# Finishing the very last output tile by column halves

The kernel's very last output tile (128 rows of 384 columns) is computed, evacuated and stored in two halves of 192 columns instead of in one piece. Everything before that tile is as it was.

## The chip, the cores and the metric

One core of a Trainium2 chip; the runs of one set share a chip, the sets were made on four different ones. The metric is the device time in microseconds of one execution; medians are of all runs, ratios of fast runs only.

## The reference, cut to what matters

```python
# attention part: gated linear recurrence, (4, 8, 768, 48) -> x of 3072 tokens x 384
for t in range(S):
    state = f[:, :, t, :, None] * state + outer(k[:, :, t], v[:, :, t])
    y[:, :, t] = q[:, :, t] @ state
# mixture part: 4 experts, 384 -> 1024 -> 384, weights p per token
for e in range(E):
    h = np.maximum(x @ w1[e], 0.0)
    out += p[:, e:e + 1] * (h @ w2[e])
```

## The kernel before

A planner places every step on an engine in simulated time and emits the instructions in that order. For each chunk of 4 x 128 tokens and each expert it computes h (8 blocks of 128 features) and then, per tile of 128 tokens, the output: 8 accumulating matmuls of 384 columns in two groups of 4, one evacuation on VectorE that adds p times the product to the tile, and, after the last expert, one store.

```python
def mm_o(c, e, nt, half):
    for fc in range(half * 4, half * 4 + 4):
        nc.tensor.matmul(out=tl("op", c, e, nt)[:, 0:Din], lhsT=tl("h", c, e)[:, fc, nt * T:(nt + 1) * T],
                         rhs=w2_sb[:, e, fc, :], start=(fc == 0), stop=(fc == KF - 1))
...
        nc.vector.scalar_tensor_tensor(out=o, in0=op, scalar=pe, in1=o, op0=ALU.mult, op1=ALU.add)
...
def store(c, nt):
    r0 = nt * S + c * T
    nc.sync.dma_start(out=out[r0:r0 + T, :], in_=tl("o", c, nt))
...
# the planner: a step whose predecessor ran on the same engine waits its lag + 0.05 us
t = max(t, d.end + d.lag + (self.LATENCY if d.engine != e else 0.05))
...
# a filler matmul is issued for every 0.2 us or so in which TensorE would idle before the first h
for _ in range(o.pad):
    nc.tensor.matmul(out=spare[:, 0:256], lhsT=busy[:, 0:128], rhs=busy, start=True, stop=True)
```

Of the kernel before, what the change touches and what calls it, by code (L numbers as in the profile page):

```python
# [99 lines left out]
def kernel(  # L100
# [11 lines left out]
    nc = tc.nc  # L112
    B, H, S, D = q.shape
    assert (B, H, S, D) == (4, 8, 768, 48)
    T = 128
    C = S // T
# [4 lines left out]
    E, Din, F = moe_w1.shape  # L121
    KD = Din // 128
    KF = F // 128
# [12 lines left out]
    P = Plan(rooms)  # L136
# [14 lines left out]
    for nm, nb in (("gp", 2), ("qk", 2)):  # L151
# [6 lines left out]
        out=mask01, in_=mask01, compare_op=ALU.is_ge, fill=0.0,  # L158
# [13 lines left out]
    w2_sb = wpool.tile([128, E, KF, Din], BF16)  # L172
# [17 lines left out]
    def tl(kind, *key):  # L190

        if (kind, key) not in tiles:
            room = kind if kind in rooms else "ps_m" if kind in ("hp", "op") else "ps_t"
            slot = P.slot[(room, kind) + key if room.startswith("ps_") else (room,) + key]
            if room in ("gp", "qk"):
                tiles[kind, key] = pads[room, slot]
            else:
                shape, dt = shapes[kind]
                pool = ps if room.startswith("ps_") else wk
                tiles[kind, key] = pool.tile(shape, dt, name=f"{room}{slot}")  # L200
        return tiles[kind, key]
# [149 lines left out]
        else:  # L351
            nc.scalar.activation(out=dst, in_=src, func=AF.Relu)  # L352

    def mm_o(c, e, nt, half):
        for fc in range(half * 4, half * 4 + 4):
            nc.tensor.matmul(out=tl("op", c, e, nt)[:, 0:Din], lhsT=tl("h", c, e)[:, fc, nt * T:(nt + 1) * T],  # L356
                             rhs=w2_sb[:, e, fc, :], start=(fc == 0), stop=(fc == KF - 1))

    def ev_o(c, e, nt, eng):
        op, o = tl("op", c, e, nt)[:, 0:Din], tl("o", c, nt)  # L360
        pe = pn[:, nt * C + c, e:e + 1]
        if e > 0:
            nc.vector.scalar_tensor_tensor(out=o, in0=op, scalar=pe, in1=o, op0=ALU.mult, op1=ALU.add)  # L363
        elif eng == "ACT":
            nc.scalar.activation(out=o, in_=op, func=AF.Copy, scale=pe)  # L365
        else:
            nc.vector.tensor_single_scalar(out=o, in_=op, scalar=pe, op=ALU.mult)  # L367

    def store(c, nt):
        r0 = nt * S + c * T  # L370
        nc.sync.dma_start(out=out[r0:r0 + T, :], in_=tl("o", c, nt))


    ld = {}
# [96 lines left out]
    hdone, omm, oev = {}, {}, {}  # L471
# [10 lines left out]

    def add_o(c, e, nt, half):
        p = unit[0] + 0.5
        key = ("ps_m", "op", c, e, nt)
        d = [hdone[k] for k in hdone if k[:2] == (c, e) and half * 4 <= k[2] < half * 4 + 4 and k[3] <= nt * T]
        m = omm[c, e, nt] = P.add(f"o {c}.{e}.{nt}.{half}", {"PE": 0.645}, lambda _: mm_o(c, e, nt, half), p,
                                  deps=d + [wd[e, 2], omm.get((c, e, nt))], takes=[key], lag=0.2, frees=[("h", c, e)])
        if half == 1:
            ev = oev[c, e, nt] = P.add(f"ev_o {c}.{e}.{nt}", {"ACT": 0.58, "DVE": 0.56} if e == 0 else {"DVE": 0.62},  # L490
                                       lambda g: ev_o(c, e, nt, g), p - 1, deps=[m, oev.get((c, e - 1, nt)), pdone[c]],
                                       takes=[("o", c, nt)], frees=[key])
            if e == E - 1:
                P.add(f"store {c}.{nt}", {"DMA": 0.6}, lambda _: store(c, nt), p, deps=[ev], frees=[("o", c, nt)])

    attention(0, lambda b, s: -200 + 3.6 * b + s * 0.8, 1)
    ALL, LO, HI = list(range(B)), [0, 1], [2, 3]
# [2 lines left out]
    def zip_units(hs, os):  # L500
        for i in range(max(len(hs), len(os))):
            if i < len(hs):
                add_h(*hs[i])
            if i < len(os):
                add_o(*os[i])
            unit[0] += 1
# [7 lines left out]
    pdone = []  # L514
# [71 lines left out]
```

## Time and profile before

The time before is 305.67 us (median). The profiled run has a span of 303.5 us.

| what | before | how to read it |
|---|---|---|
| TensorE busy | 97% | the bound up to the last matmul |
| first h matmul | 23.04 us | ends the phase of loads and of filler matmuls |
| first evacuation of the second-to-last pair | 296.75 us | I call all up to here the front |
| from there to the end | 6.78 us | the tail, all that the change touches |

I call the last four tiles A, B, C and D. The tail holds the evacuations of A and B, then those of C and D, and their stores. The view `--windows` from the start of A's evacuation gives the tail to 0.01 us (window, length, then busy times).

```profile
296.75:303.53 6.78, 3.21 (x20) 1.72 (x18) 2.48 (x4) 0.00 (x0) 0.00 (x0) 1.00 0.32 116
```

### The profile page before, as it was taken

How to read it: one execution, taken by the hardware profiler on the slowest of the kernel's cores; microseconds unless marked ns; L12 is line 12 of the kernel's file. 1: busy time of each engine (PE TensorE's matmuls, PEld its weight loads, DVE VectorE, ACT ScalarE, POOL GpSimd, SP SyncE). 2: the span in 40 equal slices, each digit the busy share in tenths (PEclk: the TensorE clock that was granted, in tenths of full speed). 3: DMA queues.
4: the chain of work that ended last, by engine and by line, in shares of the span. 5: the costliest groups of instructions: out<-in, count | busy, mean ns of one | idle time of the engine just before them, and what ended most of it. 6: DMA issues, size and time to landing. Idle time of an engine off the chain costs nothing.

```text
span 303.5 us, 5499 instructions
## 1 busy us (share of the span) xinstructions
PE 294.5 (97%) x2104; PEld 170.5 (56%) x2135; DVE 137.8 (45%) x272; ACT 170.7 (56%) x295; POOL 95.7 (32%) x157
## 2 busy tenths in 40 slices
PE   7899999999999999999999999999999999999995
PEld 5665555567775655455555555555555555555552
DVE  6684013788853764516555344544423443201223
ACT  5767654957865444676356475345476444475430
POOL 4585200408656237423426243522432000000000
PEclk9999999999999999999999999999999999999999
DMA  7999999955993589776997877301322201100002
GB/s 156 204 185 208 208 206 190 225 90 91 215 208 82 111 165 181 170 144 120 189 178 136 213 142 151 51 13 37 92 59 51 48 14 41 73 5 2 0 0 104
DMA packets 137210, 36.08 MB, mean 119 GB/s; under 512 B 128480, under 2 KB 135648, under 8 KB 137184
## 3 DMA queue, kind: packets, MB, share of 16 engines
q1 hardware_dynamic: 131424, 29.45, 48.8%
q0 software_dynamic: 5760, 6.29, 12.5%
q8 instruction: 16, 0.26, 0.4%
q14 instruction: 10, 0.08, 0.1%
HBM read 31.51 MB, written 4.72 MB: 119 GB/s over the span
## 4 chain that ended last, share of the span: by engine, by line
PE 90%; DMA 4%; DVE 2%; POOL 1%; issue 1%; ACT 1%; DVEq 0%; ACTq 0%; POOLq 0%
PE ps_m L356 40%; PE ps_m L344 40%; DMA w_sb<-in_moe_w_dram 3%; PE ps_t L300 2%; PE ps_t L255 1%; PE ps_t L315 1%; PE ps_t L321 1%; PE ps_t L311 1%; PE ps_t L285 1%; DMA f<-in_f_logit_dram 1%; POOL qk L276 1%; PE ps_m L551 1%; DVE qk L276 1%; DVE o L363 0%; DVE AT L304 0%
## 5 line engine op out<-in xcount | busy, mean ns | idle before, releaser
L352 ACT ACTIVATE h<-ps_m 128x512 bf16<-128x512 f32 (+1 forms) x171 | 98.4, 578 | 102.7 <-PE ps_m L344 92.5
L356 PE MATMUL ps_m<-w_sb,h 128*128 128x384 bf16 x768 | 153.0, 326 | 0.2
L344 PE MATMUL ps_m<-xT,w_sb 128*128 128x512 bf16 (+1 forms) x593 | 150.4, 362 | 1.9 <-DVE o L367 0.3
L356 PEld LDWEIGHTS <-h 128*128 128x128 bf16 x768 | 72.5, 98 | 57.4
L363 DVE SCALAR_TENSOR_TENSOR o<-ps_m,pn,o 128x384 f32<-128x384 f32 x72 | 44.4, 617 | 97.2 <-PE ps_m L356 89.8
L344 PEld LDWEIGHTS <-w_sb 128*128 128x128 bf16 x624 | 59.8, 98 | 46.9 <-issue 0.7
L276 POOL TENSOR_TENSOR qk<-q,e 128x384 bf16<-128x384 f32 x19 | 22.8, 1203 | 66.7 <-ACT e L262 66.2
L304 DVE TENSOR_TENSOR AT<-ps_t,mask 128x512 bf16<-128x512 f32 x48 | 31.1, 685 | 19.3 <-PE ps_t L300 19.2
L335 POOL TENSOR_TENSOR Sf<-Sf,egs 48x192 f32<-48x192 f32 x40 | 20.4, 510 | 47.5 <-DVE Sf L328 45.5
L350 DVE TENSOR_SCALAR h<-ps_m 128x512 bf16<-128x512 f32 (+1 forms) x37 | 20.7, 573 | 22.0 <-PE ps_m L344 19.7
L276 POOL TENSOR_TENSOR qk<-k,e 128x384 bf16<-128x384 f32 x20 | 21.3, 1064 | 20.3 <-ACT e L264 13.0
L262 ACT ACTIVATE e<-ps_t 128x384 f32<-128x384 f32 x24 | 20.7, 864 | 4.6 <-PE ps_t L255 2.4
L328 DVE TENSOR_TENSOR Sf<-Sf,ps_t 48x192 f32<-48x192 f32 x40 | 14.0, 350 | 9.4 <-PE ps_t L321 8.7
L336 POOL CAST sb<-Sf 48x192 bf16<-48x192 f32 x40 | 13.6, 339 | 2.6
L551 PE MATMUL ps_m<-busy 128*128 128x256 bf16 x71 | 13.1, 332 | 1.3 <-DVE busy L140 1.3
L365 ACT ACTIVATE o<-ps_m,pn 128x384 f32<-128x384 f32 x20 | 11.6, 581 | 3.9 <-PE ps_m L356 3.1
L264 ACT ACTIVATE e<-ps_t 128x384 f32<-128x384 f32 x24 | 13.0, 541 | 0.0
L218 DVE CAST yb<-ps_t 128x384 bf16<-128x384 f32 x16 | 8.9, 556 | 7.3 <-PE ps_t L315 6.3
L247 ACT ACTIVATE ex<-f 128x768 f32<-128x768 f32 (+1 forms) x14 | 10.5, 747 | 3.0 <-DMA f<-in_f_logit_dram 3.0
L315 PE MATMUL ps_t<-vb,AT 128*128 128x48 bf16 x192 | 11.4, 184 | 0.7 <-DVE vb L218 0.7
L315 PEld LDWEIGHTS <-AT 128*128 128x128 bf16 x192 | 9.8, 97 | 2.8 <-issue 0.9
L251 ACT ACTIVATE gp<-ex 128x768 bf16<-128x768 f32 (+1 forms) x14 | 10.5, 751 | 0.4
(50 smaller groups left out, 142.6 us busy)
## 6 DMA issues: line engine op xcount, KB each, us to landing
w_sb<-in_moe_w_dram POOLq DMA_DIRECT2D x8, 768.0 KB, 18.6
out_dram<-o SPq DMA_DIRECT2D x24, 192.0 KB, 1.9
f<-in_f_logit_dram SPq DMA_DIRECT2D x10, 384.0 KB, 4.2
k<-in_k_dram SPq DMA_DIRECT2D x10, 384.0 KB, 5.3
q<-in_q_dram SPq DMA_DIRECT2D x10, 384.0 KB, 5.3
v<-in_v_dram SPq DMA_DIRECT2D x10, 384.0 KB, 5.5
f<-in_f_logit_dram SPq DMA_DIRECT2D x4, 192.0 KB, 3.8
k<-in_k_dram SPq DMA_DIRECT2D x4, 192.0 KB, 3.9
```

Of the source, the lines that this page charges most:

```text
L262: nc.scalar.activation(out=e[:, 0].rearrange("t (d h) -> t h d", d=D), in_=cs[:, 0:HD].rearrange("t (i r d) -> t r i d", r=2, d=D), func=A ...
L276: engines[eng].tensor_tensor(out=tl("qk", c, b)[:, j, :, 0:D].rearrange("t (i r) d -> t i r d", r=2), in0=tl("qk"[j], c, b // 2)[:, hh(b), ...
L304: nc.vector.tensor_tensor(out=tl("AT", c, b)[:, r].rearrange("s i t -> s (i t)"), in0=tl("A", c, b, r).rearrange("s i t -> s (i t)"), in1= ...
L315: nc.tensor.matmul(out=y[:, h * D:(h + 1) * D], lhsT=AT[:, r, i, :], rhs=vb[:, h, :], start=(c == 0), stop=True, skip_group_check=True)
L328: nc.vector.tensor_tensor(out=Sf[rows, b], in0=Sf[rows, b], in1=KV[rows, :, r, :], op=ALU.add)
L335: nc.gpsimd.tensor_tensor(out=Sf[rows, b], in0=Sf[rows, b], in1=eg, op=ALU.mult)
L344: nc.tensor.matmul(out=tl("hp", c, e, fc, n0)[:, n0:n1], lhsT=w1_sb[:, e, kk, fc * 128:(fc + 1) * 128], rhs=tl("xT", c)[:, kk, n0:n1], sta ...
L350: nc.vector.tensor_relu(out=dst, in_=src)
L352: nc.scalar.activation(out=dst, in_=src, func=AF.Relu)
L356: nc.tensor.matmul(out=tl("op", c, e, nt)[:, 0:Din], lhsT=tl("h", c, e)[:, fc, nt * T:(nt + 1) * T], rhs=w2_sb[:, e, fc, :], start=(fc == ...
L363: nc.vector.scalar_tensor_tensor(out=o, in0=op, scalar=pe, in1=o, op0=ALU.mult, op1=ALU.add)
L551: nc.tensor.matmul(out=spare[:, 0:256], lhsT=busy[:, 0:128], rhs=busy, start=True, stop=True)
```

## The change

The intent: what follows the last matmul is one evacuation and one store, and both should be half as long if the last thing to be finished is half a tile. The core of the diff:

```diff
-    def mm_o(c, e, nt, half):
-        for fc in range(half * 4, half * 4 + 4):
-            nc.tensor.matmul(out=tl("op", c, e, nt)[:, 0:Din], ...
-                             rhs=w2_sb[:, e, fc, :], start=(fc == 0), stop=(fc == KF - 1))
+    def mm_o(c, e, nt, fcs, part, cols):
+        for fc in fcs:
+            nc.tensor.matmul(out=tl("op", c, e, nt, part)[:, cols], ...
+                             rhs=w2_sb[:, e, fc, cols], start=(fc == 0), stop=(fc == KF - 1))
...
-        nc.sync.dma_start(out=out[r0:r0 + T, :], in_=tl("o", c, nt))
+        nc.sync.dma_start(out=out[r0:r0 + T, cols], in_=tl("o", c, nt)[:, cols])
...
+        by_cols = (c, e, nt) == (C - 1, E - 1, B - 1)
+        part = half if by_cols else 0
+        cols = slice(half * Din // 2, (half + 1) * Din // 2) if by_cols else slice(0, Din)
+        fcs = range(KF) if by_cols else range(half * 4, half * 4 + 4)
...
-        if half == 1:
+        if half == 1 or by_cols:
```

## The prediction

> **What bounds the kernel now.** I read the page's busy line and its chain that ended last, then the groups with their shapes, then the last 4 us in the timeline, and last the view of the DMA over the final 2 us.
>
> ```profile
> span 303.5 us, 5499 instructions
> PE 294.5 (97%) x2104; PEld 170.5 (56%) x2135; DVE 137.8 (45%) x272; ACT 170.7 (56%) x295; POOL 95.7 (32%) x157
> ...
> PE 90%; DMA 4%; DVE 2%; POOL 1%; issue 1%; ACT 1%; DVEq 0%; ACTq 0%; POOLq 0%
> ```
>
> TensorE is busy for 97% of the span and is 90% of the chain. The change removes no matmul work, so 300 of the 303.5 us can't move. All it can touch is what comes after the last matmul. That stretch is this (start, length, engine, line, operation; in brackets the idle time before and its releaser):
>
> ```profile
> 298.98 0.98 PE L356 MATMUL ps_m<-w_sb,h 128*128 128x384 bf16 x5
> 299.31 0.26 PEld L356 LDWEIGHTS <-h 128*128 128x128 bf16 x2
> 299.35 1.27 DVE L363 SCALAR_TENSOR_TENSOR o<-ps_m,pn,o 128x384 f32<-128x384 f32 x2 [1.33 <-PE ps_m L356]
> 299.99 0.98 SPq L371 DMA_DIRECT2D out_dram<-o  x2
> ```
>
> The reader is to see two evacuations back to back, then two stores. The four output tiles of the last stage (call them A, B, C, D) are not run one after the other: the plan lets the second half of a tile start only 0.25 us after its first half ends, so it takes another tile's half in between, and TensorE runs C0, D0, C1, D1, each 4 matmuls. The trace agrees: evacuations come in pairs with 1.33 us of idle VectorE before each pair, and within a pair the second starts 0.65 us after the first. C's evacuation starts at 299.35, D's at 300.00, D's ends at 300.62, D's store is issued at 300.64. The span still has 2.9 us to go there. The DMA view over 300.6 to 302.6 us, 40 slices of 0.05 us, shows what the first half of those is:
>
> ```profile
> DMA  0000477999989982105999989995410000000000
> GB/s 0 0 0 0 184 276 276 430 430 430 430 307 369 430 277 62 31 31 215 369 492 399 399 307 430 430 492 185 154 31 0 0 0 0 0 0 0 0 0 0
> DMA packets 288, 0.39 MB, mean 197 GB/s; under 512 B 32, under 2 KB 288, under 8 KB 288
> ```
>
> Slices 4 to 14 are C's store (300.80 to 301.35), 18 to 29 D's (301.50 to 302.10), so about 0.58 us of data each, nearly touching. The data begin about 0.83 us after their issue. The store lands 1.8 us after the issue, at about 302.45 (from the lines of the output's stores, quoted below), 0.35 us after the last data; then 1.0 us of semaphores and barriers closes the program.
>
> **What the Trainium skill says.**
> (1) "VectorE: DVE Perf Modes", section "The TRN2 errata": an operation costs a fixed part plus the elements per partition over the clock, 120 + 384 cycles at 0.96 GHz = 525 ns for a PSUM source. The trace agrees on the form, not on the fixed part: the operation takes 618 ns. The trace's own slope comes from two shapes of one operation (L350 below): (690 - 419) / 256 = 1.06 ns per element, so half the columns don't mean half the time.
> (2) "TensorE: Matmul & The Clock Gate", section "Back-to-back issue gap": warm matmuls follow one another at N / 2.4 + 2.5 ns, but a stream with weight loads is given as about 81 ns at N = 128. Here 4 matmuls of 384 columns take 0.65 us on the chain (162.6 ns each, the formula's 162.5), and three with 256 columns 0.325 us (108 each, formula 109), each with its own weight load. Groups of 96, 48 and 48 columns, three weight loads, repeat every 0.10 us, 33 ns per pair. So weight loads don't bound at 192 columns, and I use 192 / 2.4 + 2.5 = 82.5 ns, not a value above 81 that a weight floor would give.
> (3) "DMA: Bandwidth & Descriptors", sections "Specifications" and "Anatomy of one DMA": most of a transfer's fixed cost is the receipt of the write, which does not scale with size, and pieces should be at least 512 B. A half row is 768 B, so it stays above. The trace shows the fixed part: of 1.8 us from issue to landing only 0.58 are data.
> (4) "PSUM — Partial Sum Buffer", section "Terms": TensorE writing and VectorE reading one bank at once is an error. The change gives the halves two PSUM tiles, so D's first half can be evacuated while its second half is computed. The trace of before can't show it.
>
> ```profile
> L363 DVE SCALAR_TENSOR_TENSOR o<-ps_m,pn,o 128x384 f32<-128x384 f32 x72 | 44.4, 617 | 97.2 <-PE ps_m L356 89.8 <-ACT h L352 6.3
> L350 DVE TENSOR_SCALAR h<-ps_m 128x512 bf16<-128x512 f32 x21 | 14.4, 690 | 19.6 <-PE ps_m L344 17.3 <-ACT e L262 1.9
> L350 DVE TENSOR_SCALAR h<-ps_m 128x256 bf16<-128x256 f32 x16 | 6.4, 419 | 2.4 <-PE ps_m L344 2.4
> ```
>
> ```profile
> L371 SPq DMA_DIRECT2D out_dram<-o x4: 332/332/332, 297.4 to 300.6; - x4
> ...
> DMA to landing us min/median/max: 1.8/1.9/1.9
> ```
>
> **The change part by part.**
> Matmuls: D's 8 of 384 columns become 16 of 192. 16 x 82.5 = 1320 ns against 8 x 162.6 = 1301: +0.02 us, all on the path. Eight more weight loads lie beside them. The order stays C0, D0, C1, D1, since priorities and planned lengths of the matmul steps stay; only D0 and D1 now mean left and right columns.
> First half of D, new work: its evacuation can start when D0 ends, about 298.67 (C1's end at 299.32 less 0.65). It takes 618 - 192 x 1.06 = 415 ns, to 299.1, inside the 1.33 us in which VectorE idles. Its store is issued at about 299.13 (0.33 us of a free queue) and its data move at about 299.95 to 300.3, when the engines are idle. None of that is on the path.
> Second half of D: evacuation 415 instead of 618 ns: -0.20 us, on the path. It starts at about 300.02 and ends at 300.43; the store is issued at about 300.46 instead of 300.64. C's store has been issued by 300.32, so the queue is free.
> Its data: to estimate the time of a packet I take two points. All loads and stores of the hardware queue: 48.8% of 16 engines' 303.5 us over 131424 packets, 18 ns at 224 B on average. The four last stores: 28.6% of 16 engines' 7.5 us over 576 packets is 34.3 us; less 64 small ones at 18 ns, 65 ns for each of 512 rows of 1536 B. The line through both gives 37 ns for 768 B, 0.58 of a full row. So D's data take about 0.34 us, not 0.58. They could begin at 300.46 + 0.83 = 301.29, but C's are moving until 301.38 or so, so the engines finish both at about 301.38 + 0.34 = 301.72. Before, they finished at 302.10: -0.38 us.
> This last number already holds the 0.20 of the evacuation, because the path runs through it: 0.18 of an earlier issue plus 0.24 of shorter data, less 0.04 to 0.05 of collision with C's data. The receipt and the closing 1.0 us stay. I choose -0.35 us, a little less than the sum, since the slope through the packets mixes loads and stores: 305.67 - 0.35 = 305.32 us.
>
> **The rivals.**
> (a) The stored half is bound by packets and not by bytes: eight rows per engine stay eight rows, and data stay near 0.58 us. The 18 ns for small packets speak against. Then D's data end at 301.38 + 0.58 = 301.96, and the gain is 0.14 us: 305.53.
> (b) A new wait takes the place of the old: D's right half may only be written into the output tile, or stored, once the store of the left half has landed, if the halves are taken to overlap. The left store lands at about 299.13 + 1.8 = 300.93. If only the second store waits, it is issued at 300.95 instead of 300.64, and the gain is gone (+0.31 - 0.24 = +0.07): 305.75. If the evacuation waits, another 0.4 comes on top: 306.2. Against it: the strided slices of one transposed tile (L293's transfers) show no waits for one another among the queue's waits. All stores of before write whole rows, so the output itself is untested. I give both forms 15% together.
> (c) D0's evacuation comes behind C's in VectorE's order. Then D1's would wait for it, 299.97 + 0.42 + 0.42 = 300.8, worse by 0.2. The plan places by readiness, and D0 ends 0.65 us before C1, so I give it 3%.
> (d) A weight load binds the 192-column matmuls at the 98 ns of its own duration: 16 x 98 = 1568, +0.27 us on the path, which eats most of the gain: 305.6. The 33 ns spacing speaks against.
>
> **Range and chances.** All rivals lie within 0.6 us of 305.67, about 0.2%, while one of the three runs of before was 0.55 us above the others. The lower end is the full gain with nothing lost, 0.2 + 0.25, and 0.2 of scatter: 305.0. The upper end is rival (b) or a run of the higher kind less the gain, 305.95. Within 2% (6.1 us) is all but certain; what is left is for a shifted plan or a layout effect that I don't see.
>
> **What would show it.** Right: L363 twice with 192 columns at about 415 ns, the first of them before C's; 16 matmuls of 192 columns at 82 ns spacing; 25 stores instead of 24, the last issued at about 300.46; its data joined to C's without a gap and ended at about 301.7; span about 303.15. Wrong: a wait of the store queue for a landing, or of VectorE for a transfer, at the end (b); data of about 0.6 us for the half (a); matmuls at 98 ns (d); any shift before 297 us, where the schedules should be the same.

## The result, and the profile after

The changed kernel took 305.01 us (median of six runs), with fast runs of 304.54, 304.54, 304.97 and 305.06 and two slow ones of 314.95 and 316.14. The ratio to before is 0.9972, with a 95% interval of 0.9952 to 0.9992. A ratio is formed from the fast runs of both kernels, so it isn't quite the ratio of the medians. It stands for 0.86 us (0.0028 of the 305.6 us mean of before), where I had forecast 0.35: more than twice as much. All outputs are right.

The page's first lines (span, busy time by engine, the chain that ended last) show a span that is 0.8 us shorter.

```profile
span 302.7 us, 5517 instructions
PE 293.2 (97%) x2112; PEld 169.4 (56%) x2143; DVE 138.1 (46%) x273; ACT 170.8 (56%) x295; POOL 95.5 (32%) x157
...
PE 88%; DMA 4%; DVE 2%; SPq 2%; issue 1%; POOL 1%; ACT 1%; DVEq 0%; ACTq 0%; POOLq 0%
```

The timeline of the tail after the change (start, length, engine, line, operation; idle time and releaser in brackets):

```profile
296.38 1.27 DVE L363 SCALAR_TENSOR_TENSOR o<-ps_m,pn,o 128x384 f32<-128x384 f32 x2 [1.33 <-PE ps_m L356]
298.33 0.42 DVE L363 SCALAR_TENSOR_TENSOR o<-ps_m,pn,o 128x192 f32<-128x192 f32 x1 [0.69 <-PE ps_m L356]
298.99 1.08 DVE L363 SCALAR_TENSOR_TENSOR o<-ps_m,pn,o 128x384 f32<-128x384 f32 x2 [0.23 <-PE ps_m L356]
```

The left half of D (298.33) fits into what was idle time, C follows, and the right half ends at 300.07. Its store is issued at 300.09, 3.71 us after A's evacuation began; before, it was 300.64 less 296.75, 3.89 us. The DMA view over 300.3 to 302.3 us, 40 slices of 0.05 us, shows C's and D's data without a gap:

```profile
GB/s 0 0 0 215 307 369 399 338 461 492 338 369 369 338 338 323 415 338 308 139 46 0 0 0 0 0 0 0 0 0 0 0 0 0 0 0 0 0 0 0
DMA packets 288, 0.30 MB, mean 148 GB/s; under 512 B 32, under 2 KB 288, under 8 KB 288
```

The data end at 301.35 us; the store lands (the profile shows its completion) 1.6 us after its issue, 1.8 before. From the last issue to the end are 2.62 us, 2.89 before. The tail as a whole:

```profile
296.38:302.70 6.33, 3.23 (x28) 2.29 (x26) 2.69 (x5) 0.00 (x0) 0.00 (x0) 0.96 0.36 127
```

So the span's 0.8 us divides in two. The tail went from 6.78 to 6.33 us, a gain of 0.45: 0.18 from the earlier issue and 0.27 from the smaller store. But A's evacuation itself began 0.37 us earlier, where the two programs still do the same (up to it, the two traces list the same instructions in the same order on every engine). To see where that comes from, the chain of waits of the first 30 us, before and after (start, length, what):

```profile
13.60 1.31 POOL qk L276
14.91 8.08 DMA w_sb<-in_moe_w_dram
22.99 0.04 issue
23.04 0.39 PE ps_m L344
```

```profile
13.03 1.36 POOL qk L276
14.38 0.25 issue
14.63 8.07 DMA w_sb<-in_moe_w_dram
22.70 0.05 issue
22.74 0.39 PE ps_m L344
```

The first weights are asked for 0.28 us sooner and the first h matmul starts 0.30 us sooner. GpSimd issues this load, after a product of its own (L276) and, by an order that the kernel sets, after the last load of k has landed. Before, the product ended last, at 14.91 us. After, it started 0.57 us sooner, and the issue came 0.31 us after the landing of k (14.32 us in the trace). Of what lies ahead of the product, the chain before holds twelve of the filler matmuls, and the chain after doesn't (timeline of TensorE, before and after):

```profile
5.49 2.72 PE L551 MATMUL ps_m<-busy 128*128 128x256 bf16 x12
```

```profile
5.35 1.47 PE L556 MATMUL ps_m<-busy 128*128 128x256 bf16 x12
```

The twelve take nearly twice as long before as after: TensorE reached its full pace earlier in the profile after. The page's granted clock is full in both, so it doesn't show this; durations do. The skill's page "TensorE: Matmul & The Clock Gate", section "What's actually happening", says that the array runs at half pace until a free-running activity window of 3.4 us has been busy, and that the number of slow matmuls therefore varies from run to run. That agrees with what the runs below show, in that the same twelve took 1.47 or 2.72 us in profiles of one program; no run here shows the window itself. I had not taken it into the prediction.

All sixteen profiles fit this reading. In the six in which the twelve fillers took 2.72 us, the product started at 13.56 to 13.66 us and the weights were asked for as it ended, at 14.87 to 15.03. In the other ten it started at 12.62 to 13.15, and the weights were asked for 0.30 to 0.31 us after k had landed, at 14.52 to 15.06. By this reading slow fillers cost the profile of before about 0.3 us (14.91 instead of 14.31, where k landed, plus 0.31). Without them the landing of k sets the issue, and that scatters by itself (14.21 to 14.76 us in the ten). The chain of a copy of the changed kernel (change_third_time, below) shows the second case:

```profile
10.22 4.18 DMA k<-in_k_dram
14.40 0.30 issue
14.70 8.35 DMA w_sb<-in_moe_w_dram
```

This is read from the traces. No experiment set the pace of the fillers or the landing of k.

### The profile page after: what moved, and what is told of

The parts are those of the page before. It is cut to its first block, busy times and chain, and to the rows that moved or that the text cites. A ratio compares the mean times of both kernels' runs of the same rounds, so it can differ in the third digit from the quotient of the medians.

```text
span 302.7 us, 5517 instructions
## 1 busy us (share of the span) xinstructions
PE 293.2 (97%) x2112; PEld 169.4 (56%) x2143; DVE 138.1 (46%) x273; ACT 170.8 (56%) x295; POOL 95.5 (32%) x157
## 3 DMA queue, kind: packets, MB, share of 16 engines
q0 software_dynamic: 5760, 6.29, 12.4%
## 4 chain that ended last, share of the span: by engine, by line
PE 88%; DMA 4%; DVE 2%; SPq 2%; issue 1%; POOL 1%; ACT 1%; DVEq 0%; ACTq 0%; POOLq 0%
PE ps_m L356 41%; PE ps_m L344 40%; DMA w_sb<-in_moe_w_dram 3%; PE ps_t L300 2%; SPq L222 2%; DMA f<-in_f_logit_dram 1%; PE ps_t L315 1%; PE ps_t L321 1%; PE ps_t L311 1%; PE ps_t L255 1%; PE ps_t L285 1%; DVE qk L276 1%; POOL qk L276 0%; DVE AT L304 0%; POOL Sf L335 0%
## 5 line engine op out<-in xcount | busy, mean ns | idle before, releaser
L363 DVE SCALAR_TENSOR_TENSOR o<-ps_m,pn,o 128x384 f32<-128x384 f32 (+1 forms) x73 | 44.6, 611 | 96.8 <-PE ps_m L356 89.4
L276 POOL TENSOR_TENSOR qk<-q,e 128x384 bf16<-128x384 f32 x19 | 22.8, 1204 | 64.9 <-ACT e L262 64.4
L276 POOL TENSOR_TENSOR qk<-k,e 128x384 bf16<-128x384 f32 x20 | 21.0, 1052 | 19.8 <-ACT e L264 12.9
L556 PE MATMUL ps_m<-busy 128*128 128x256 bf16 x71 | 11.5, 301 | 1.3 <-DVE busy L140 1.3
```

Source lines behind the costliest of these rows:

```text
L276: engines[eng].tensor_tensor(out=tl("qk", c, b)[:, j, :, 0:D].rearrange("t (i r) d -> t i r d", r=2), in0=tl("qk"[j], c, b // 2)[:, hh(b), ...
```

## The experiments

Theory: the change gains what the tail gains, 0.45 us, and the rest of the first measurement is scatter of the front. Rival: the changed program also shifts its front. The same copies were then used to take the tail apart. In the table, "issued" is the time from the start of A's evacuation to the issue of the last store, and "to the end" from there to the end of the span. The quoted texts use 6.75 and 6.32 us for the two tails, from a span that is rounded to 0.1 us; I use the finer figures.

| kernel | issued, us | to the end, us | tail, us |
|---|---|---|---|
| before | 3.89 | 2.89 | 6.78 |
| changed | 3.71 | 2.62 | 6.33 |
| same_again | 3.89 | 2.90 | 6.79 |
| same_third_time | unknown | 3.89 | 2.90 | 6.79 |
| change_again | 3.72 | 2.60 | 6.32 |
| change_third_time | unknown | 3.79 | 2.67 | 6.46 |
| halves_one_store | 3.71 | 2.91 | 6.62 |
| store_split_only | 4.28 | 2.68 | 6.96 |
| right_256 | 3.78 | 2.68 | 6.46 |
| right_128 | 3.89 | 2.58 | 6.47 |
| third_first | 3.72 | 2.58 | 6.30 |
| third_first_again | unknown | 3.72 | 2.57 | 6.29 |
| thirds | 3.99 | 2.48 | 6.47 |
| thirds_two_queues | 3.67 | 2.44 | 6.11 |
| change_fewer_fillers | unknown | 3.71 | 2.62 | 6.33 |
| before_more_fillers | unknown | 3.89 | 2.90 | 6.79 |

Some profiles fell in a slow state of 311 to 315 us. Their lost time lies in the loads: the first h matmul starts at 30 to 33 us in the slow ones, at 23 to 24 in the fast. The tail of one and the same kernel is alike in both to 0.01 us (6.78 and 6.79 before, 6.33 and 6.32 changed; the one exception, change_third_time, is explained below), and the granted clock over the tail is 0.93 to 1.00, so I read their tails.

**same_again** (nothing changed)

> The kernel of before, unchanged. I split each run's span into a front (start of the span to the start of the first evacuation of the second-to-last pair, 296.75 us before and 296.38 us after) and a tail (from there to the end, 6.75 and 6.32 us). Theory: the change gains only 0.43 us, in the tail; the other 0.4 us of the first measurement came from scatter of the front, in the load phase. Then this copy gives a ratio of 1.000 with an interval of some 0.002, a tail of 6.75 within 0.03, and a front that differs from 296.75 by up to 0.5 us. Rival: the front belongs to the program; then the front is 296.75 within 0.1.

The ratio of this unchanged copy was 1.0033, with an interval of 0.9989 to 1.0077. Its fast runs went from 304.87 to 309.32 us, and the eleven runs of before beside it from 304.83 to 306.54. That is wider than I had expected, and several times the 0.35 us that I wanted to see. The profile was slow, but its start already contradicts the rival:

```profile
5.30 1.47 PE L551 MATMUL ps_m<-busy 128*128 128x256 bf16 x12
```

This is the program of before with the fillers of the changed one, and it issued its first weights at 14.56 us.

**change_again** (nothing changed against the changed kernel)

> The changed kernel, unchanged. Theory (gain in the tail alone): ratio 0.9986 within 0.001, tail 6.32 within 0.03, front anywhere within 0.5 us of the other copies'. Rival (the changed program also shifts its front, for instance by another layout of buffers or instructions): ratio 0.997 again, and a front near 296.4 while the copy of before has 296.75.

The ratio was 0.9986 (0.9959 to 1.0012), the theory's number, but the interval holds the rival's too. The tail, 6.32, is the theory's.

**same_third_time** and **change_third_time**

> The kernel of before once more, one look, for a second front of the unchanged program in the fast state. In the profile of before, 12 of the filler matmuls in the first 9 us took 2.7 us and the weight load was issued at 14.91 us; in that of the changed kernel they took 1.5 us and it was issued at 14.63, and the first hidden-layer matmul came 0.30 us sooner. Theory: that is chance and not the program. Then this run shows one or the other (fillers of 1.5 to 2.7 us, issue at 14.5 to 15.0), not tied to 14.91 and 2.7; the tail is 6.75. Rival (the program sets it): 2.7 us, 14.9.

> The changed kernel once more, one look. Theory: tail 6.32 again, fillers and weight load anywhere in the same range as the copy of before. Rival: fillers 1.5 us and an issue at 14.6 again.

The unchanged kernel had fillers of 1.47 us this time, weights issued at 15.06 us and its first h matmul at 25.55; its tail was 6.79. The changed one had 1.47, 14.70 and 23.10. So the program of before had slow fillers once (2.72 us) and fast ones twice (1.47). The changed program had fast ones in all three profiles, but third_first, whose edit lies in the last tile too, had 1.88 us in one profile and 2.72 in the other. The filler time doesn't belong to a program. Nor do fast fillers alone give an early start: in this copy of the changed kernel the weights were asked for at 14.70 but took 8.35 us, and in the unchanged one the first h matmul waited for the last load of v, which landed at 22.10. From the first h matmul to A's evacuation the four profiles agree within 0.1 us (273.6 to 273.7), so the scatter lies ahead of it. The front of one program scatters by about the 0.37 us in question or more: 296.38 and 296.74 us in two profiles of the changed kernel, 296.75 and 299.16 in two of before. The tail of this changed copy was 6.46 instead of 6.33; that question is taken up at the end of this section.

**halves_one_store** (the second half of the change undone)

```diff
+                if by_cols and half == 0:
+                    return
-                ... lambda _: store(c, nt, cols) ...
+                ... lambda _: store(c, nt, slice(0, Din)) ...
```

> Columns halved for matmuls and evacuation, but one whole store after the second evacuation. Theory: the evacuation alone gives its 0.20 us less 0.02 for the matmuls, but C's data are still moving when D's could begin, and D's take the whole 0.58 us, so the tail shortens by 0.14 to 0.18 us against before (6.57 to 6.61). Rival (all of the gain lies in the evacuation, the smaller store is hidden by the fixed cost of landing): tail 6.35.

The ratio was 0.9986 (0.9967 to 1.0006), which tells nothing apart. The tail was 6.62 us, 0.01 above the theory's range and far from the rival's 6.35. The last issue stands at 3.71, as in the changed kernel, and what follows takes 2.91, about as before. So the two terms come apart: the half evacuation alone shortens the tail by 0.16 us, the half store by another 0.29.

**store_split_only** (the kernel of before, the last store alone divided)

```diff
+        cuts = [slice(0, Din // 2), slice(Din // 2, Din)] if (c, nt) == (C - 1, B - 1) else [slice(0, Din)]
+        for cols in cuts:
-            nc.sync.dma_start(out=out[r0:r0 + T, :], ...)
+            nc.sync.dma_start(out=out[r0:r0 + T, cols], ...)
```

> The kernel of before with only its last store split into two column halves, issued one behind the other. Theory: the second issue comes 0.33 us later, its data take 0.34 instead of 0.58 us and begin 0.83 us after their issue, so the data end 0.04 to 0.10 us later than before: tail 6.75 to 6.85. Rival (what counts is only that the last transfer is small): tail 6.5.

The tail was 6.96, longer than before by 0.18; both guesses were too low. (The ratio, 0.9995 with 0.9973 to 1.0016, tells nothing.) The second issue came 0.39 us after the first (301.04 and 301.43), and only 0.21 of that came back from the smaller transfer. Dividing the store alone doesn't pay here: its last part was not issued earlier.

**right_256** and **right_128** (the cut moved)

```diff
-        cols = slice(half * Din // 2, (half + 1) * Din // 2) if by_cols else slice(0, Din)
+        CUTS = [0, 128, 384]          # right_128: [0, 256, 384]
+        cols = slice(CUTS[half], CUTS[half + 1]) if by_cols else slice(0, Din)
```

> The changed kernel with columns cut 128 and 256 instead of 192 and 192. Theory: the last evacuation takes 618 - 128 x 1.06 = 482 ns (64 more than in the changed kernel) and the data 0.42 instead of 0.34 us; C's data still end first. Tail 0.12 to 0.15 us longer than the changed kernel's 6.32: 6.44 to 6.47. Rival (the store's time does not scale with its size): tail 6.39.

> Columns cut 256 and 128. Theory: the last evacuation takes 347 ns and the last data 0.26 us, but it queues behind C's evacuation and behind C's data: C's store data end the same, so the end comes 0.08 us (data) to 0.15 us (data and evacuation) before the changed kernel's: tail 6.17 to 6.24. A risk on VectorE: the right part's matmuls take only 0.45 us after C1's end while C's evacuation takes 0.62, so the last evacuation starts 0.15 us after its matmuls end. That would put the tail at 6.24 to 6.30. Rival (a fixed floor of landing): 6.30.

The ratios, 0.9919 (0.9804 to 1.0035) and 0.9952 (0.9862 to 1.0043), are as wide as the scatter of before beside them (305.34 to 309.46). With 256 columns on the right the tail was 6.46, as the theory had it. With 128 it was 6.47, and I had said 6.17 to 6.30. What follows the last issue shrinks with the size (2.89 us with 384 columns, 2.68 with 256, 2.62 with 192, 2.58 with 128). But with 128 the last evacuation ended at 301.34 us and its store was issued only at 301.53: C's store, issued at 301.11, was still being issued on the same queue.

**third_first** and **third_first_again** (C finished whole before D begins)

```diff
+        if by_cols and half == 0:
+            d.append(omm[c, e, nt - 1])
```

> The halves of the change, with the third tile C finished whole before D begins (C0, C1, D0, D1). Theory: C's data are out of the way 0.65 us earlier, so D's right half moves as soon as it can: the collision of 0.04 to 0.09 us in the sum goes. Tail 6.23 to 6.28. Rival (no collision in fact): tail 6.32.

> The order C0, C1, D0, D1 again, because its first profile fell in the slow state: tail 6.35 there. Theory now (the collision of C's and D's data costs nothing measurable): 6.32 to 6.35 again. Rival (the slow state hid a gain): 6.23 to 6.28.

The tails were 6.30 (slow) and 6.29, against 6.32, 6.33 and 6.33 in change_again, the changed kernel and change_fewer_fillers (below). The last issue came as before (3.72), so the difference of 0.02 to 0.04 us lies behind it, where the collision should be. That is near the 0.04 to 0.05 us of my sum. It is small against all else here, and only the finer figures show it: with a span rounded to 0.1 us, as in the second expectation, it can't be seen.

**thirds** and **thirds_two_queues** (C first, D in three parts of 128 columns; then with the stores of C and of D's middle part on ScalarE's queue)

```diff
+        CUTS = [0, 128, 256, 384]
+    zip_units([], ol(C - 1, E - 1, ALL) + [(C - 1, E - 1, B - 1, i) for i in range(2, 3)])
     # thirds_two_queues
+        eng = nc.scalar if (c, e, nt) == (C - 1, E - 1, B - 2) or by_cols and part == 1 else nc.sync
+        eng.dma_start(...)
```

> C finished first, then D in three parts of 128 columns, each evacuated and stored by itself. Theory: last evacuation 347 instead of 418 ns (-0.07), last data 0.26 instead of 0.34 us (-0.08), without collision (-0.04 to -0.09), 24 matmuls at 56 ns instead of 16 at 82 (+0.02). Tail 6.10 to 6.17. Rival (weight loads bind the 128-column matmuls at some 80 ns): +0.6 us in the matmuls, tail about 6.7.

> D in three parts of 128 columns with C first, as before, but the stores of C and of D's middle part are issued by ScalarE's queue, so no two stores follow one another on one queue within 0.9 us. In the earlier run with thirds the last evacuation ended 3.64 us into the tail and its store was issued only at 3.99, because the stores stood in line on one queue about 0.45 us apart. Theory (that line is why thirds gained nothing): the last store is issued at 3.66 to 3.70 and the tail is 6.14 to 6.25, 0.1 to 0.2 us under the changed kernel's. Rival (it isn't the queue but the descriptors or the data that stand in line): 6.45 again.

Thirds gained nothing: 6.47, and a ratio of 0.9931 (0.9843 to 1.0020) that tells nothing. The four stores were issued at 307.52, 307.95, 308.42 and 308.92 us, though the last evacuation had ended at 308.57. With two queues the last issue stood at 3.67 instead of 3.99 and the tail at 6.11 us, as the theory of the queue had it and a little below its range. The timeline shows the two queues at work:

```profile
299.20 1.69 DVE L363 SCALAR_TENSOR_TENSOR o<-ps_m,pn,o 128x384 f32<-128x384 f32 x4 [0.68 <-PE ps_m L356]
299.85 0.96 ACTq L371 DMA_DIRECT2D out_dram<-o  x2
```

The tail of this version is 0.67 us shorter than before's and 0.22 us shorter than the changed kernel's. Its total was 305.13 us (ratio 0.9961, interval 0.9906 to 1.0015). The scatter of the front hides the gain, so I don't call it faster by the clock.

**change_fewer_fillers** and **before_more_fillers.** In change_third_time the store of B held its queue for 1.44 us instead of 0.33, so that D's first store was issued at 299.57 us although its evacuation had ended at 299.12, and the last one 0.07 us late. A's and B's stores landed after 3.0 us. The stores of that tail:

```profile
L371 SPq DMA_DIRECT2D out_dram<-o x5: 332/395/1436, 297.4 to 300.5; - x5
DMA to landing us min/median/max: 1.7/1.9/3.0
```

The page of every kernel with divided columns lists 17 blocks on the instruction queue q8, that of before 16. One of them moved at 297 to 299 us in the fast profiles. The two experiments change only the number of fillers:

```diff
+    left = -12        # before_more_fillers: +8
+    for o in reversed(done):
+        if o.pad and left:
+            d = max(left, -o.pad) if left < 0 else left
+            o.pad, left = o.pad + d, left - d
```

> The changed kernel with 12 of its 71 filler matmuls (and their weight loads) left out before the first hidden-layer matmul, so that its TensorE stream is 8 instructions shorter than that of before instead of 16 longer. Theory: the 17th block of instructions, which all kernels with divided columns fetched at 297 to 299 us and before did not, is TensorE's and goes away: 16 blocks again, the stores of tiles A and B land in 1.9 us, each store's issue takes 0.33 us, and the tail is 6.31. Rival (the block is another engine's, or the slow landings come from the divided stores): 17 blocks or landings of 2.5 to 3.0 us again.

> The kernel of before with 8 more filler matmuls (16 more TensorE instructions, as many as the change adds). Theory: a 17th block is fetched in the tail, A's and B's stores land in 2.1 to 3.0 us instead of 1.9, the last two as before or a little later; tail 6.75 to 6.90. Rival: 16 blocks, landings of 1.9, tail 6.75.

Without the 12 fillers the changed kernel had 16 blocks, every issue took 0.33 to 0.34 us, no landing was over 1.9, and the tail was 6.33:

```profile
q8 instruction: 16, 0.26, 0.3%
```

```profile
L371 SPq DMA_DIRECT2D out_dram<-o x5: 332/333/344, 306.6 to 309.7; - x5
DMA to landing us min/median/max: 1.6/1.8/1.9
```

The kernel of before with 8 fillers more did have 17 blocks, as expected, but the landings stayed at 1.9 and the tail at 6.79: half of that theory was wrong. There the block moved at 299.3 to 300.3 us, ahead of A's evacuation at 300.47 and so ahead of any store. So the block follows the length of TensorE's instructions, and in the tail slow landings were seen only where it met the first stores. That it causes them is argued from this meeting; no run moved the block alone. Stores earlier in the kernel land slowly too (3.1 us for the one issued at 216.42 us before), which I didn't follow up. The skill's page "Runtime: NRT & Kernel Launch", section "Instruction fetch mechanics", says that an engine's instructions come in 16 KiB blocks and that the cost of a block is mostly hidden. Here it is mostly hidden too: the tail is 6.33 us without a block in it, 6.33 with one and an issue of 0.94, 6.32 with an issue of 0.61, 6.46 with one of 1.44.

## Why the prediction was right or wrong, point by point

- **The tail's mechanism: right.** D's left half was evacuated and stored in idle time, no new wait appeared (rival b), the order of evacuations was the one predicted (rival c), and the right half's path was shorter in both its parts. One expectation of point (4) didn't come about: the left half was evacuated (298.33 to 298.75 us) while TensorE worked on C, before D's right half began at 298.78. In third_first_again the two did run side by side.
- **The matmuls: right.** From 293.74 us to the end of the last matmul at 299.62 run 28 matmuls of 384 columns and 16 of 192. 5.88 us less 28 x 162.6 ns leaves 83 ns for each of the 16, where I had 82.5. Rival d falls.
- **The evacuation: right.** 418 ns measured, 415 predicted; the issue came 0.18 us earlier, as predicted.
- **The store: right in size.** The last store landed 1.84 us after its issue before and 1.63 after (to 0.01 us in the trace): 0.21 less, where I had 0.24 for its data less 0.04 for the collision. Rival a falls.
- **The collision: about right.** I took off 0.04 to 0.05 us for C's data; third_first shows 0.02 to 0.04.
- **The closing: wrong, small.** "The receipt and the closing 1.0 us stay" didn't hold. From the landing of the last store to the end of the span the traces show 1.04 us in the three profiles of before and 0.97 to 0.99 in the three of the changed kernel; with one whole store at the end (halves_one_store) it is 1.04 again. So it goes with the half store, and why is open. The tail's gain is then 0.18 + 0.21 + 0.06 = 0.45 us, where I had 0.38 and chose 0.35.
- **Point (3) of the prediction.** The figures of the profile of before say that of the 1.84 us about 0.83 lie ahead of the data and 0.35 to 0.4 behind.
- **The step that failed is the last one:** "The lower end is the full gain with nothing lost, 0.2 + 0.25, and 0.2 of scatter". It rests on "300 of the 303.5 us can't move", and the front did move. The scatter is that of the front, and it was mis-sized. The unchanged kernel's fast runs spread over 1.7 us beside each other in one set of rounds, and its copy's over 4.4. The first comparison (0.86 us) holds 0.45 of the change, 0.30 from an earlier first h matmul (its weights were asked for 0.28 us sooner), 0.07 more from the front, and the rest is the difference between the profiled runs and the mean. A second comparison gave 0.9986, or 0.4 us. That the second number is near the tail's 0.45 is partly luck, since its interval is wider than that.
- **A check of mine was wrong as well:** "any shift before 297 us, where the schedules should be the same" was to count against the prediction. The programs are the same there, their times are not.
- **What stays open:** whether some of the front belongs to the program. The program of before shows both filler times and issues its weights at 14.56 to 15.06 us, which holds the changed program's 14.63 to 14.70, so no run shows a shift tied to the change. In all profiles the issue of the weights follows the later of two events, the end of GpSimd's product and the landing of k, and both move from run to run. But three profiles of each are few, the changed program's all had the fast fillers, and no interval here is narrow enough to exclude 0.2 us. Why the fast runs of before reach 309 us in some rounds was not followed up.

## What to carry to other kernels

A kernel that is busy to its last matmul ends with one evacuation, one store and a fixed rest, and dividing the last tile shortened the first two by their variable parts only: here 0.45 us of 305. Finer parts paid here only where each store found a free queue, since stores on one queue went out some 0.4 to 0.5 us apart. When the gain is smaller than the start-up's scatter, compare stretches of traces from a common event instead of total times, and run an unchanged copy first.

## What the Trainium skill lacked or had wrong

- "TensorE: Matmul & The Clock Gate", "Back-to-back issue gap": about 81 ns is given for a stream of matmuls with weight loads at N = 128. Here 24 matmuls of 128 columns, each with its own weight load, took 56 ns each (5.90 us of the chain less 28 x 162.6 ns, over 24), and those of 192 columns 83 ns. The simple formula holds; the weight loads were hidden.
- "VectorE: DVE Perf Modes", "The TRN2 errata": 120 cycles plus the elements gives 525 ns for 384 columns from PSUM and 325 ns for 192. Measured were 618 and 418 ns for the operation with two tensors and a scalar: the slope is right and the fixed part is about 93 ns more.
- "Runtime: NRT & Kernel Launch", "Instruction fetch mechanics": a block of instructions is called mostly hidden. It says nothing of DMA stores that move meanwhile. Here stores that met a block in the tail landed after 2.1 to 3.0 instead of 1.9 us, and the issuing queue was held for up to 1.44 instead of 0.33 us.
- No page that I read has the pace at which one queue takes small stores: 0.38 to 0.50 us from one to the next when they stood in line.
